# Softmax with the row maximum: scores on four banks, another bank order in the query bursts, the first 28 tiles normalized on GpSimd

## The chip, the cores and the metric

The kernel runs on one core of a Trainium2 chip. The time is the device time of one execution in microseconds (us), as the median of several runs. The engines are named as in the profile: PE (TensorE's matmuls; PEld are its weight loads), DVE (VectorE), ACT (ScalarE), POOL (GpSimd), and SP, which issues most of the DMAs.

## The reference

A layer norm of x (2048 rows of 448) feeds an attention over the last 512 positions of a cached K and V (16 query heads of 256, two to each of 8 K/V heads) and a gated feed-forward block (1792 wide). The output is x + attention * silu(feed-forward).

```python
W = min(4096, max(256, Sk // 4))                       # 512
q = (x @ wq).reshape(B, Sq, Hq, Dh).transpose(0, 2, 1, 3)
k = jnp.repeat(k_cache[:, :, Sk - W:, :], rep, axis=1)
v = jnp.repeat(v_cache[:, :, Sk - W:, :], rep, axis=1)
scores = jnp.einsum("bhqd,bhkd->bhqk", q, k) * (Dh ** -0.5)
p = softmax(scores, axis=-1)
o = jnp.einsum("bhqk,bhkd->bhqd", p, v)
s = o.transpose(0, 2, 1, 3).reshape(B, Sq, Hq * Dh) @ wo
g = silu((gelu(x @ w_gate) * (x @ w_up)) @ w_down)
out = x_in + s * g                                     # x above is layernorm(x_in)
```

## The kernel before

The author's recorder `Rec` takes the instructions in program order, finds the dependencies by key and puts semaphore waits in front of an instruction where it needs them. Each engine runs its own instructions strictly in the recorded order; there is no scheduler. A PSUM bank is a key `("ps", b)`: who writes a bank waits for all earlier readers of it.

The 2048 rows are four blocks of 512. First comes the feed-forward for all four (`gate_up`, `down`), with the layer norm of the next block between; the last block's `down` is kept back and its 56 matmuls are spread as pieces over the first score tiles (the table `fill`). Then comes the attention: a loop over `i` from 0 to 63, one head of one block each (head i % 16 of block i // 16), and within it over four tiles `t` of 128 rows. Tile number n is 4 i + t.

In one turn of the inner loop, `scores(i, t)` multiplies 128 query rows with the 512 keys: two matmuls (L552) into one bank, 4 or 5 in turn. ACT takes the exponential straight from the bank, with the scale folded in, and sums the row (L556); DVE forms the reciprocal of the sum (L558) and multiplies the row by it (L559). The normalized tile, in one of 11 buffers `pr`, is transposed by a DMA issued from SP (`dmaT`) into `pT`. No row maximum is subtracted.

At t = 0 and 2, from tile 12 on, `values` (L574) multiplies an earlier head's transposed probabilities with V, about three heads behind, into bank 0, 1 or 6; a DVE copy (L581) moves the result to `oT`. At t = 1 and 3, from head 7 on, half of an output projection (`outproj`, L604) runs into bank 7, and after the second half DVE adds the bank to `acc` (L627; L625 for the first group of a block). When a block's last group is added, POOL multiplies with the gate `gy` and adds x (L631, L633). Three heads are other than the rest: at i = 18, 34 and 50 the values give way to the projection of a second row tile (bank 6), and at i = 22, 38 and 54 there is no projection. The last head of each block is folded (its V and its part of wo were multiplied beforehand, `vw`) and needs no `values`. The gate's tanh runs on ACT (L645) with two POOL steps (L646, L648) after heads 7, 9, 11 and 13 of a block.

The queries come in bursts: `q_burst` runs at tile t = 0 of head 3 (four heads) and of heads 7, 15, 23, 31, 39, 47 and 55 (eight heads), after that turn's scores and values. A burst of eight heads has eight parts, each for two heads and one half of the 256 columns. A part uses a pair of banks, s and s + 1, and has two phases: eight matmuls of 64 rows that run in pairs, and six more. PE's order puts the first phase of part n ahead of the second phase of part n - 1:

```python
for n in range(heads + 1):
    if n < heads:
        part(n, 0)
    if n:
        part(n - 1, 1)
```

After a part's second phase ACT copies both banks to `qT` in one instruction of 1024 columns (L527). The pairs are taken as `2 * (n % 3)` in the bursts of eight: banks 0 and 1, 2 and 3, 4 and 5, 0 and 1, and so on. In the burst at head 3 the pairs are 0, 2, 1, 0.

Of the kernel before, what the change touches and what calls it, by code (L numbers as in the profile page):

```python
# [5 lines left out]
ACT = mybir.ActivationFunctionType  # L6
ALU = mybir.AluOpType
BF16 = mybir.dt.bfloat16
F32 = mybir.dt.float32

LN_EPS = 1e-5
P = 128
# [132 lines left out]
def bass_recurrent_scan__sliding_block_cached__geglu_ffn__prompt_kernel(nc, A_x, A_k, A_v, A_wq, A_wo, B_x, B_wg, B_wu, B_wd, out):  # L145
    _, S, D = A_x.shape
# [3 lines left out]
    W = min(4096, max(256, Sk // 4))  # L150
    F = B_wg.shape[1]
    QC, TPC, HP, KF = 512, 4, 64, 3
# [5 lines left out]
    scale = float(Dh) ** -0.5  # L158
# [3 lines left out]
    with es:  # L162
        off = [16512]

        def sb(name, shape, dt, at=None):
            n = 4 if dt == F32 else 2
            for x in shape[1:]:
                n *= x
            if at is None:
                at = off[0]  # L170
                off[0] += (n + 31) // 32 * 32
            return R.place(name, shape, dt, at), at + (n + 31) // 32 * 32

        ident, _ = sb("ident", [P, P], BF16)
        small, _ = sb("small", [P, 4], F32)
        stats, _ = sb("stats", [P, NT, 6], F32)
        mv, _ = sb("mv", [P, NT, 2], F32)
        std, _ = sb("std", [P, NT], F32)
        rstd, _ = sb("rstd", [P, NT], F32)
        den, _ = sb("den", [P, 16], F32)  # L180
        rden, _ = sb("rden", [P, 16], F32)

        xnT, _ = sb("xnT", [P, NQC, KF + 1, QC], BF16)
        gy, _ = sb("gy", [P, NT, D], BF16)
        kT, _ = sb("kT", [P, Hkv, NE, W], BF16)
        V, _ = sb("V", [P, NJ, Hkv, Dh], BF16)

        wq, _ = sb("wq", [P, KF, Hq, Dh], BF16)
        wq6, _ = sb("wq6", [P, Hq // 2, Dh], BF16)
        wo, _ = sb("wo", [P, Hq * NE, D], BF16)  # L190

        vw, _ = sb("vw", [P, NJ, D], BF16)
        gu_at = off[0]

        wg, _ = sb("wg", [P, KF, F], BF16)
        wu, _ = sb("wu", [P, KF, F], BF16)
        wgu6, x_at = sb("wgu6", [P, F], BF16)
        x4, _ = sb("x4", [P, NT, D], BF16)
        NX = 4
        xn2, d_at = sb("xn2", [P, NX, D + HP], BF16)  # L200
        wd, _ = sb("wd", [P, NF, D], BF16)
# [13 lines left out]
        pr = []  # L215
# [17 lines left out]
        NPR = len(pr)  # L233
        psum = es.enter_context(nc.psum_tensor("ps", [P, 8 * 512], F32))

        def bank(b, n=512):
            return psum[:, b * 512:b * 512 + n]
# [6 lines left out]
        act = lambda *a, **k: R.op("scalar", *a, **k)  # L244
        dve = lambda *a, **k: R.op("vector", *a, **k)
        pool = lambda *a, **k: R.op("gpsimd", *a, **k)
# [4 lines left out]
        def dmaT(dst, src, w=(), r=(), after=(), lane=None):  # L251
# [9 lines left out]
             r=[("ident",)], w=[("ident",)])  # L261
# [245 lines left out]
        NI = NQC * Hq  # L507
        NG = NI // 4

        def q_slot(i):  # L510

            p = i // 2
            p = p if p < 3 else (p - 3) % NQP
            return qT[p], "qT%d" % p, i % 2

        def q_burst(i0, heads):

            c, h0 = divmod(i0, Hq)

            def part(n, ph):  # L520
                hp, e_ = divmod(n, 2)
                s, h = 2 * (n % 3 if heads == 8 else (0, 2, 1, 0)[n] if i0 else (n + 2) % 4), h0 + 2 * hp
                buf, name, _ = q_slot(i0 + 2 * hp)
                two_blocks(ph, c, s, [wq[:, :, h + m, e_ * P:(e_ + 1) * P] for m in range(2)],
                           wq6[:, h // 2, e_ * P:(e_ + 1) * P], wq_keys)
                if ph:
                    act(lambda e: e.activation(  # L527
                        buf[:, :, e_, :], psum[:, s * 512:(s + 2) * 512].rearrange("p (a q) -> p a q", a=2), ACT.Copy),
                        r=[("ps", s), ("ps", s + 1)], w=[(name, e_)])

            for n in range(heads + 1):
# [5 lines that stand above are left out]
        def folded(i):  # L537
            return i % Hq == Hq - 1

        def p_slot(i):  # L540

            n = (i - i // Hq) % NPT
            return (pTf, ("pT", "f")) if folded(i) else (pT[:, n, :, :], ("pT", n))

        def scores(i, t):
            g, n = (i % Hq) // 2, i * TPC + t
            b, s = 4 + n % 2, n % NPR
            buf, name, a = q_slot(i)

            def run(e):  # L550
                for k in range(NE):
                    ins = e.matmul(bank(b), lhsT=buf[:, a, k, t * P:(t + 1) * P], rhs=kT[:, g, k, :],  # L552
                                   start=k == 0, stop=k == NE - 1)
                return ins
            pe(run, r=[("kT", g), (name, 0), (name, 1)], w=[("ps", b)])
            act(lambda e: e.activation(pr[s][:, :], bank(b), ACT.Exp, scale=scale, accum_out=den[:, s:s + 1]),  # L556
                r=[("ps", b)], w=[("pr%d" % s,), ("den", s)])
            dve(lambda e: e.reciprocal(rden[:, s:s + 1], den[:, s:s + 1]), r=[("den", s)], w=[("rden", s)])  # L558
            dve(lambda e: e.tensor_scalar(pr[s][:, :], pr[s][:, :], rden[:, s:s + 1], None, op0=ALU.mult),  # L559
                r=[("pr%d" % s,), ("rden", s)], w=[("pr%d" % s,)])  # L560
            dst, key = p_slot(i)
            dmaT(dst[:, :, t * P:(t + 1) * P], pr[s][:, :], r=[("pr%d" % s,)], w=[(*key, t)], lane="p%d" % s)

        def values(i, e_):
            g = (i % Hq) // 2
            idx = (i % 4) * NE + e_
            src, pkey = p_slot(i)
            at = 2 * i + e_ + 6

            b = (0, 6, 0, 6, 0, 1, 6, 6)[at % 8] if at < 2 * NI else (0, 6, 1, 0, 6, 1)[at - 2 * NI]  # L570

            def run(e):
                for j in range(NJ):
                    ins = e.matmul(bank(b), lhsT=V[:, j, g, e_ * P:(e_ + 1) * P], rhs=src[:, j, :],  # L574
                                   start=j == 0, stop=j == NJ - 1)
                return ins
            pe(run, r=[(*pkey, t) for t in range(TPC)] + ([("V", j) for j in range(NJ)] if g < Hkv - 1 else [("V", "f")]),
               w=[("ps", b)])
            dst, key = oT[(i // 4) % 2][:, idx, :], ("oT%d" % ((i // 4) % 2), idx)
            if i < NI - 2:  # L580
                dve(lambda e: e.tensor_copy(dst, bank(b)), r=[("ps", b)], w=[key])  # L581
            else:
                act(lambda e: e.activation(dst, bank(b), ACT.Copy), r=[("ps", b)], w=[key])

        def n_pieces(G):
            return 3 * NE + NJ if folded(4 * G + 3) else 4 * NE
# [55 lines left out]
        def silu(n):  # L642

            s = n % 2
            act(lambda e: e.activation(tmp[:, s, :], gy[:, n, :], ACT.Tanh, scale=0.5), r=[("gy", n)], w=[("tmp", s)])  # L645
            pool(lambda e: e.tensor_scalar(tmp[:, s, :], tmp[:, s, :], 1.0, 0.5, op0=ALU.add, op1=ALU.mult),  # L646
                 r=[("tmp", s)], w=[("tmp", s)])
            pool(lambda e: e.tensor_tensor(gy[:, n, :], tmp[:, s, :], gy[:, n, :], ALU.mult),  # L648
                 r=[("tmp", s), ("gy", n)], w=[("gy", n)])


        for c in range(NQC):
            lead = 6 if c == 0 else 2
            for f in range(NF + 1):
# [4 lines left out]
                t = (f - lead) // 2  # L659
# [17 lines left out]
        load_xr(0)  # L677

        fill = {}
        for d, slots in ((0, range(0, 4)), (1, range(4, 12)), (2, range(13, 17)), (3, range(17, 21))):  # L680
            for n, s in enumerate(slots):
                fill[s] = d, range(n * NF // len(slots), (n + 1) * NF // len(slots))
        pv = [(i, e_) for i in range(NI) if not folded(i) for e_ in range(NE)]
        outs = [(G, t) for G in range(NG) for t in range(TPC)]
        for i in range(NI):
            for t in range(TPC):
                scores(i, t)
                if 4 * i + t in fill:
                    down(NQC - 1, *fill[4 * i + t])

                early = i >= Hq and i % Hq == 2
                if t % 2 == 0 and early:
                    n = n_pieces(outs[1][0])
                    outproj(*outs[1], range(n * t // 4, n * (t + 2) // 4), b=6)
                elif t % 2 == 0 and 4 * i + t >= 12:
                    values(*pv.pop(0))
                if 7 <= i and t % 2 and not (i >= Hq and i % Hq == 6):
                    n = n_pieces(outs[0][0])
                    outproj(*outs[0], range(n * (t - 1) // 4, n * (t + 1) // 4))
                    if t == TPC - 1:  # L700
                        del outs[0:1 + early]
                if t == 0 and (i == 3 or i % 8 == 7) and i + 1 < NI:
                    q_burst(i + 1, 4 if i == 3 else 8)
            if i % Hq in (7, 9, 11, 13):
                silu(i // Hq * TPC + (i % Hq - 7) // 2)

        for what in "vvovovo":
            if what == "v":
# [38 lines left out]
```

## Time and profile before

| what | value |
|---|---|
| median of 3 runs | 558.33 us (558.14 to 558.38) |
| the profiled execution | 558.53 us, of it 556.7 us span |
| last block's feed-forward ends, attention begins | 133.5 us |
| first tile's exponential; tile 12's; tile 28's; tile 255's | 134.77; 144.60; 170.23; 537.47 us |
| a burst of eight heads, 170.9 to 183.1 us | PE 12.20, DVE 1.13, ACT 6.77 us busy of 12.20 |
| the run of 31 tiles after it, 183.1 to 222.9 us | PE 39.49, DVE 31.41, ACT 25.00, POOL 6.40 us busy of 39.80 |
| the granted TensorE clock | 1.00 throughout |
| exponential, L556, 128x512 | 598 ns, 256 of them |
| batch statistics, L335, 128x448 on DVE | 619 ns |
| POOL product of two tiles, L631, 128x448 | 1035 ns |

The page's times are those of one profiled execution. A duration is that of one instruction from start to end; on one engine the end of one overlaps with the start of the next, so that an engine's durations can add up to more than it needs. "Idle before" says how long an engine stood still before the instructions of a group, and which instruction ended it. The windows of the table are sums of busy time of the engine in that stretch.

### The profile page before, as it was taken

How to read it: one execution, taken by the hardware profiler on the slowest of the kernel's cores; microseconds unless marked ns; L12 is line 12 of the kernel's file. 1: busy time of each engine (PE TensorE's matmuls, PEld its weight loads, DVE VectorE, ACT ScalarE, POOL GpSimd, SP SyncE). 2: the span in 40 equal slices, each digit the busy share in tenths (PEclk: the TensorE clock that was granted, in tenths of full speed). 3: DMA queues.
4: the chain of work that ended last, by engine and by line, in shares of the span. 5: the costliest groups of instructions: out<-in, count | busy, mean ns of one | idle time of the engine just before them, and what ended most of it. 6: DMA issues, size and time to landing. Idle time of an engine off the chain costs nothing.

```text
span 556.7 us, 9892 instructions
## 1 busy us (share of the span) xinstructions
PE 550.0 (99%) x3517; PEld 261.4 (47%) x3550; DVE 313.7 (56%) x822; ACT 296.1 (53%) x689; POOL 88.6 (16%) x125
## 2 busy tenths in 40 slices
PE   9999999999999999999999999999999999999997
PEld 6444444444444444444444444444444444444445
DVE  5535436043463678077728744772688077628774
ACT  5333324237655666555575556556665655575640
POOL 0131213200000121002301110131121002311134
PEclk9999999999999999999999999999999999999999
DMA  8883555952444354245554552556355245635461
GB/s 237 287 141 70 134 86 96 265 114 54 97 86 76 58 100 96 53 85 96 128 76 93 104 92 42 96 99 139 66 96 102 41 87 103 138 64 105 95 96 52
DMA packets 165440, 57.65 MB, mean 104 GB/s; under 512 B 155648, under 2 KB 162304, under 8 KB 165392
## 3 DMA queue, kind: packets, MB, share of 16 engines
q1 hardware_dynamic: 162048, 44.64, 42.5%
q0 software_dynamic: 3040, 12.16, 8.1%
q8 instruction: 28, 0.46, 0.3%
q10 hardware_dynamic: 304, 0.22, 0.2%
q14 instruction: 20, 0.16, 0.1%
HBM read 17.92 MB, written 1.84 MB: 35 GB/s over the span
## 4 chain that ended last, share of the span: by engine, by line
PE 98%; DMA 1%; issue 1%; SPq 0%; DVE 0%
PE ps L472 33%; PE ps L552 20%; PE ps L574 19%; PE ps L604 19%; PE ps L496 8%; DMA V<-in_A_v_cache_dram 1%; PE ps L400 0%; PE ps L357 0%; PE ps L387 0%; PE ps L347 0%; SPq L249 0%; PE ps L359 0%; DVE tmp L615 0%; DVE xr L617 0%
## 5 line engine op out<-in xcount | busy, mean ns | idle before, releaser
L556 ACT ACTIVATE pr<-ps 128x512 bf16<-128x512 f32 x256 | 152.6, 598 | 120.1 <-PE ps L552 118.8
L552 PE MATMUL ps<-kT,qT 128*128 128x512 bf16 x487 | 145.2, 379 | 2.3 <-issue 1.4
L558 DVE RECIPROCAL rden<-den 128x1 f32<-128x1 f32 x256 | 41.4, 162 | 154.1 <-ACT pr L556 139.6
L574 PE MATMUL ps<-pT,V 128*128 128x512 bf16 x472 | 121.9, 379 | 0.4
L559 DVE TENSOR_SCALAR pr<-pr,rden 128x512 bf16<-128x512 bf16 x256 | 106.1, 414 | 9.0
L604 PE MATMUL ps<-wo,oT 128*128 128x448 bf16 (+1 forms) x498 | 110.9, 346 | 0.0
L472 PE MATMUL ps<-xnT,wq 64*128 64x512 bf16 x896 | 98.3, 376 | 0.0
L527 ACT ACTIVATE qT<-ps 128x1024 bf16<-128x1024 f32 x64 | 64.6, 1023 | 43.3 <-PE ps L472 43.0
L472 PE MATMUL ps<-xnT,wu 64*128 64x512 bf16 x336 | 82.3, 376 | 0.0
L472 PE MATMUL ps<-xnT,wg 64*128 64x512 bf16 x336 | 82.0, 376 | 0.0
L581 DVE CAST oT<-ps 128x512 bf16<-128x512 f32 x118 | 80.5, 683 | 0.7 <-PE ps L574 0.6
L490 DVE TENSOR_TENSOR actT<-ps,hb 128x512 bf16<-128x512 f32 x56 | 38.5, 692 | 65.9 <-ACT hb L489 61.7
L552 PEld LDWEIGHTS ps<-kT,qT 128*128 128x128 bf16 x512 | 49.2, 98 | 55.4 <-issue 4.0
L574 PEld LDWEIGHTS ps<-pT,V 128*128 128x128 bf16 x480 | 47.0, 98 | 56.3
L604 PEld LDWEIGHTS ps<-wo,oT 128*128 128x128 bf16 x498 | 48.4, 98 | 48.6 <-DVE acc L627 1.0
L472 PEld LDWEIGHTS ps<-xnT,wq 64*128 64x128 bf16 x896 | 43.0, 94 | 54.5 <-DVE rden L558 1.7
L489 ACT ACTIVATE hb<-ps 128x512 bf16<-128x512 f32 x56 | 33.1, 594 | 38.6 <-PE ps L472 38.5
L556 ACT ACTIVATION_READ_ACCUMULATOR pr<-ps 128x1 f32 x256 | 50.3, 196 | 0.0
L496 PE MATMUL ps<-wd,actT 128*128 128x448 bf16 x224 | 46.2, 353 | 0.0
L472 PEld LDWEIGHTS ps<-xnT,wg 64*128 64x128 bf16 x336 | 31.3, 94 | 20.5 <-issue 1.1
L472 PEld LDWEIGHTS ps<-xnT,wu 64*128 64x128 bf16 x336 | 31.3, 94 | 19.9
L646 POOL TENSOR_SCALAR tmp<-tmp 128x448 f32<-128x448 f32 x16 | 9.0, 565 | 198.1 <-ACT tmp L645 198.1
(60 smaller groups left out, 264.7 us busy)
## 6 DMA issues: line engine op xcount, KB each, us to landing
pT<-pr SPq DMA_TRANSPOSE x240, 2.5
wq<-in_A_wq_dram POOLq DMA_DIRECT2D x14, 256.0 KB, 3.7
wo<-in_A_wo_dram POOLq DMA_DIRECT2D x3, 896.0 KB, 8.3
V<-in_A_v_cache_dram POOLq DMA_DIRECT2D x4, 448.0 KB, 7.0
xr<-in_A_x_dram POOLq DMA_DIRECT2D x4, 448.0 KB, 4.1
wd<-in_B_w_down_dram SPq DMA_DIRECT2D x1, 1568.0 KB, 14.3
x<-in_A_x_dram SPq DMA_DIRECT2D x3, 448.0 KB, 7.5
out_dram<-xr POOLq DMA_DIRECT2D x3, 448.0 KB, 3.7
```

What stands on the lines that cost most here:

```text
L472: ins = e.matmul(bank(s + m)[:, q0:q1], lhsT=lhsT, rhs=xnT[lo:lo + HP, c, k, q0:q1], start=ph == 0 and k == 0, stop=ph == 1 and k == KF - 1)
L489: act(lambda e: e.activation(hb[:, h, :], bank(s), ACT.Gelu_apprx_tanh), r=[("ps", s)], w=[("hb", h)])
L490: dve(lambda e: e.tensor_tensor(actT[:, f, :], bank(s + 1), hb[:, h, :], ALU.mult), r=[("ps", s + 1), ("hb", h)], w=[("actT", f)])
L496: pe(lambda e, f=f: e.matmul(bank(b, D), lhsT=actT[:, f, t * P:(t + 1) * P], rhs=wd[:, f, :], start=f == 0, stop=f == NF - 1), r=[("actT", ...
L527: act(lambda e: e.activation(buf[:, :, e_, :], psum[:, s * 512:(s + 2) * 512].rearrange("p (a q) -> p a q", a=2), ACT.Copy), r=[("ps", s), ...
L552: ins = e.matmul(bank(b), lhsT=buf[:, a, k, t * P:(t + 1) * P], rhs=kT[:, g, k, :], start=k == 0, stop=k == NE - 1)
L556: act(lambda e: e.activation(pr[s][:, :], bank(b), ACT.Exp, scale=scale, accum_out=den[:, s:s + 1]), r=[("ps", b)], w=[("pr%d" % s,), ("de ...
L558: dve(lambda e: e.reciprocal(rden[:, s:s + 1], den[:, s:s + 1]), r=[("den", s)], w=[("rden", s)])
L559: dve(lambda e: e.tensor_scalar(pr[s][:, :], pr[s][:, :], rden[:, s:s + 1], None, op0=ALU.mult), r=[("pr%d" % s,), ("rden", s)], w=[("pr%d ...
L574: ins = e.matmul(bank(b), lhsT=V[:, j, g, e_ * P:(e_ + 1) * P], rhs=src[:, j, :], start=j == 0, stop=j == NJ - 1)
L581: dve(lambda e: e.tensor_copy(dst, bank(b)), r=[("ps", b)], w=[key])
L604: ins = e.matmul(bank(b, D)[:, lo:hi], lhsT=lhsT, rhs=rhs, start=idx == 0, stop=idx == n8 - 1)
```

## The change

Each score tile now has its row maximum taken by DVE from the bank, negated (`nmax`), and ACT's exponential gets it as its bias; the scale moves into the copy of the queries. The reciprocal and the multiplication of a tile are taken out of `scores` into `normalize`, which is called one tile later (LAG = 1). For the first 28 tiles POOL does the multiplication. The scores use three banks (4, 5, 2) up to tile 12 and then four (2 to 5) in turn. The copies of the attention values go to ACT, except the odd half of heads 0 to 6. The pairs of banks in the bursts and the slots of the kept-back `down` pieces have another order.

```diff
+        nmax, _ = sb("nmax", [P, 16], F32)
...
-                s, h = 2 * (n % 3 if heads == 8 else (0, 2, 1, 0)[n] if i0 else (n + 2) % 4), h0 + 2 * hp
+                s, h = 2 * ((2, 0, 1, 2, 0, 2, 1, 0)[n] if heads == 8 else (0, 1, 2, 0)[n] if i0 else (n + 2) % 4), h0 + 2 * hp
...
-                        buf[:, :, e_, :], psum[:, s * 512:(s + 2) * 512].rearrange("p (a q) -> p a q", a=2), ACT.Copy),
+                        buf[:, :, e_, :], psum[:, s * 512:(s + 2) * 512].rearrange("p (a q) -> p a q", a=2), ACT.Copy, scale=scale),
...
+        LAG, FIRST = 1, 7 * TPC
+
+        def s_bank(n):
+            return (4, 5, 2)[n % 3] if n <= 3 * TPC else 2 + (n + 1) % 4
+
         def scores(i, t):
             g, n = (i % Hq) // 2, i * TPC + t
-            b, s = 4 + n % 2, n % NPR
+            b, s = s_bank(n), n % NPR
...
-            act(lambda e: e.activation(pr[s][:, :], bank(b), ACT.Exp, scale=scale, accum_out=den[:, s:s + 1]),
-                r=[("ps", b)], w=[("pr%d" % s,), ("den", s)])
+            dve(lambda e: e.tensor_reduce(nmax[:, s:s + 1], bank(b), mybir.AxisListType.X, ALU.max, negate=True),
+                r=[("ps", b)], w=[("nmax", s)])
+            act(lambda e: e.activation(pr[s][:, :], bank(b), ACT.Exp, bias=nmax[:, s:s + 1], accum_out=den[:, s:s + 1]),
+                r=[("ps", b), ("nmax", s)], w=[("pr%d" % s,), ("den", s)])
+
+        def normalize(i, t):
+            s = (i * TPC + t) % NPR
             dve(lambda e: e.reciprocal(rden[:, s:s + 1], den[:, s:s + 1]), r=[("den", s)], w=[("rden", s)])
-            dve(lambda e: e.tensor_scalar(pr[s][:, :], pr[s][:, :], rden[:, s:s + 1], None, op0=ALU.mult),
-                r=[("pr%d" % s,), ("rden", s)], w=[("pr%d" % s,)])
+            if i * TPC + t < FIRST:
+                pool(lambda e: e.tensor_tensor(pr[s][:, :], pr[s][:, :], rden[:, s:s + 1].to_broadcast([P, W]), ALU.mult),
+                     r=[("pr%d" % s,), ("rden", s)], w=[("pr%d" % s,)])
+            else:
+                dve(lambda e: e.tensor_scalar(pr[s][:, :], pr[s][:, :], rden[:, s:s + 1], None, op0=ALU.mult),
+                    r=[("pr%d" % s,), ("rden", s)], w=[("pr%d" % s,)])
             dst, key = p_slot(i)
             dmaT(dst[:, :, t * P:(t + 1) * P], pr[s][:, :], r=[("pr%d" % s,)], w=[(*key, t)], lane="p%d" % s)
...
-            if i < NI - 2:
+            if i * TPC < FIRST and e_:
                 dve(lambda e: e.tensor_copy(dst, bank(b)), r=[("ps", b)], w=[key])
             else:
                 act(lambda e: e.activation(dst, bank(b), ACT.Copy), r=[("ps", b)], w=[key])
...
-        for d, slots in ((0, range(0, 4)), (1, range(4, 12)), (2, range(13, 17)), (3, range(17, 21))):
+        for d, slots in ((0, range(0, 4)), (1, range(4, 8)), (2, range(8, 12)), (3, range(13, 23))):
...
             for t in range(TPC):
+                n = i * TPC + t
                 scores(i, t)
+                if n >= LAG:
+                    normalize(*divmod(n - LAG, TPC))
...
+        for n in range(NI * TPC - LAG, NI * TPC):
+            normalize(*divmod(n, TPC))
```

## The prediction

> **What bounds the kernel now.** I read the page's busy times first, then its chain of waits, then the groups by line, then the timelines of one burst of query projections (L472, L527) and of one stretch of score tiles.
>
> ```profile
> span 556.7 us, 9892 instructions
> ...
> PE 550.0 (99%) x3517; PEld 261.4 (47%) x3550; DVE 313.7 (56%) x822; ACT 296.1 (53%) x689; POOL 88.6 (16%) x125
> ...
> PE 98%; DMA 1%; issue 1%; SPq 0%; DVE 0%
> ...
> L558 DVE RECIPROCAL rden<-den 128x1 f32<-128x1 f32 x256 | 41.4, 162 | 154.1 <-ACT pr L556 139.6
> L559 DVE TENSOR_SCALAR pr<-pr,rden 128x512 bf16<-128x512 bf16 x256 | 106.1, 414 | 9.0
> L527 ACT ACTIVATE qT<-ps 128x1024 bf16<-128x1024 f32 x64 | 64.6, 1023 | 43.3 <-PE ps L472 43.0
> L581 DVE CAST oT<-ps 128x512 bf16<-128x512 f32 x118 | 80.5, 683 | 0.7 <-PE ps L574 0.6
> ```
>
> PE is the chain: 98% of it, with every other engine near half busy. A busy share alone does not prove a dense PE, so I checked the distance from one matmul's start to the next: 216 ns for 512 columns and 189 ns for 448, in the run of score tiles without exception other than a few missing records. So the change can hardly win time; it can lose it wherever PE, which works strictly in order, meets a bank that is not free. Three places matter.
>
> First, the bursts. Eight parts of queries are projected in a row; each is a first half (8 matmuls in 4 pairs, 0.863 us) and, after the next part's first half, a second half (3 pairs, 0.648 us), then one copy of 1024 columns on ACT empties its two banks.
>
> ```profile
> 381.14 1.02 ACT L527 ACTIVATE qT<-ps 128x1024 bf16<-128x1024 f32 x1 [2.51 <-PE ps L472]
> 382.65 1.02 ACT L527 ACTIVATE qT<-ps 128x1024 bf16<-128x1024 f32 x1 [0.49 <-PE ps L472]
> 384.16 1.02 ACT L527 ACTIVATE qT<-ps 128x1024 bf16<-128x1024 f32 x1 [0.49 <-PE ps L472]
> ```
>
> The copies come every 1.51 us = 0.863 + 0.648 and ACT idles 0.49 us before each. The trace has the second half's last pair starting at 380.72 us and the next pair at 380.94, so the copy (381.14) begins 0.205 us after PE could take up the next thing, and ends 1.229 us after it.
>
> Second, what PE does when it must wait for such a copy; there is one such place already, after the small burst of the fourth head:
>
> ```profile
> 150.97 1.94 ACT L527 ACTIVATE qT<-ps 128x1024 bf16<-128x1024 f32 x2 [0.49 <-PE ps L472]
> ...
> 152.04 0.30 PEld L496 LDWEIGHTS ps<-wd,actT 128*128 128x128 bf16 x3 [0.43 <-ACT qT L527]
> 152.05 0.74 PE L496 MATMUL ps<-wd,actT 128*128 128x448 bf16 x3
> ```
>
> The first of the two merged copies ends at 151.99 (150.97 + 1.02) and the matmul that writes its bank starts at 152.05: release to matmul takes about 0.05 us.
>
> Third, VectorE in a run of score tiles, where it has room today:
>
> ```profile
> 341.70 0.35 DVE L559 TENSOR_SCALAR pr<-pr,rden 128x512 bf16<-128x512 bf16 x1
> 341.97 0.68 DVE L581 CAST oT<-ps 128x512 bf16<-128x512 f32 x1
> ...
> 343.23 0.62 DVE L627 TENSOR_TENSOR acc<-ps,acc 128x448 f32<-128x448 f32 x1
> ```
> ```profile
> 364.57 0.77 DVE L559 TENSOR_SCALAR pr<-pr,rden 128x512 bf16<-128x512 bf16 x1
> 365.26 0.68 DVE L581 CAST oT<-ps 128x512 bf16<-128x512 f32 x1
> 365.86 0.15 DVE L558 RECIPROCAL rden<-den 128x1 f32<-128x1 f32 x1
> ```
>
> Durations overlap, so I count slots, start to start with nothing waited for: 0.27 us for the multiply (341.70 to 341.97), 0.60 for a 512-column read from PSUM (365.26 to 365.86), 0.20 for a reciprocal and the wait of the multiply behind it, 0.53 for the 448-column accumulation (L627).
>
> **The change part by part.** The sum is against the profiled execution: 558.53 us, 1.83 above its span. The median of the runs shown, 558.33, is 0.2 lower; I carry that as nothing.
>
> *The maximum.* 256 reductions of 128x512 from PSUM on DVE, none in the trace. Nearest row: the CAST, same shape and source. Lower bound of its slot 0.52 (512 elements at the slope between the 448- and 512-column CASTs, 618 and 683 ns: 65 ns for 64), upper 0.68 (the CAST's duration without overlap). I take 0.60, the CAST's slot, since the batch statistics (L335), also a reduction, take 619 ns for 448, what the 448-column CAST takes.
>
> *What DVE loses in exchange.* 111 of the 118 output CASTs of L581 move to ACT; DVE keeps seven, the odd halves of heads 0 to 6. A head of four tiles then costs DVE 4 x (0.60 + 0.20 + 0.27) + 0.53 = 4.81 us. PE takes 4.97 for a head in a run (two tiles 2.485, the starts of L552 at 341.41 and 343.89). So it fits with 0.16 to spare. I also walked the order of the queue, for a lateness hidden in the mean. The accumulation that frees bank 7 stands behind the reduction and the multiply of the tile before; by the slots it starts 0.51 us after PE ends the projection, ends at 1.13, and PE wants the bank at about 1.5 (today it starts at 0.63 and PE does not wait). At 0.60 it costs nothing; cover left 0.3 us. Should the reduction take 0.68, a head is 5.13, 0.16 over PE, and the runs (seven of about eight heads, each restarting with an empty queue after a burst) lose 7 x (8 x 0.16 - 0.3) = 6.9 us. At 0.52 nothing changes.
>
> In the head with two accumulations (18, 34, 50) and the head before a burst without any projection (22, 38, 54) DVE is over PE by 0.2 and 0.8 us; four score banks take that up, but the burst behind the second starts on banks 4 and 5, whose last exponential by my walk ends within 0.2 us of its turn. I put 0.2 each, 3 x 0.2 = 0.5 with the smaller ones, bounds 0 and 3.
>
> [...]
>
> *ACT.* Today exponential to exponential takes 0.48 + 0.09 us. A bias read from a tile adds 93 ns (L373, one column with such a bias, 296 ns; the one without, L675, 203). So two tiles cost ACT 2 x 0.66 + one output copy 0.48 (the slot of L489) = 1.80 of 2.485 us. Hidden; the exponential now waits for the reduction, some 0.7 us, but the bank is wanted four tiles later instead of two. The scale moved into the copy of L527 is the same instruction.
>
> *The multiply one tile later; the first 28 on POOL.* 28 products of 512 columns at 1035 x 512/448 = 1.18 us (L631); bounds 0.65 (L646, one input, 565 ns scaled alike) and 1.6 (with the 0.42 by which a product of POOL and a multiply of DVE hold each other up in the line above). With the gap of 0.08 it is 35 us beside 37 us of PE (133.5 to 170.9). The first values, at tile 12, have their last product done some 1.6 us before at the middle price, hidden; at 1.6 the cover is 0.3. Its transposes wait on SP behind it in order: SP issues one in 1.21 us and a tile takes 1.24, as today. Tile 28 of each burst is normalized only behind the burst; its head is wanted nine tiles later.
>
> POOL's products hold up the multiply today (0.77 instead of 0.35 in the line above, L631 running). [...]
>
> *The banks of the bursts: here it costs.* The pairs of banks were taken in the order 0 1 2 0 1 2 0 1: a part reuses the pair of the part three before, whose copy has 1.51 us, and needs 1.229 + 0.05 = 1.28. Now the order is 2 0 1 2 0 2 1 0. Sixth part on pair 2, as the fourth: only two apart. In PE's order the sixth part's first half stands directly behind the fourth part's second half, so that the whole copy lies bare: PE waits 1.28 us. PE has nothing else in its queue to put there. Seven bursts of eight parts (heads 7, 15, ..., 55): 7 x 1.28 = 8.9 us. Bounds: 7 x 1.229 = 8.6 with no release time, 7 x 1.43 = 10.0 with 0.2, the longest that a load of L552 waited for an exponential. The other parts stay three or more apart.
>
> In the burst of four at head 3 the order becomes 0 1 2 0, and the next score tile takes bank 4, of the third part. Its first matmul moves from 151.52 (by its weight load; the record of the matmul is missing) to about 152.05, and the 0.09 us of today's wait, shown above, falls away: 0.45 us.
>
> *Down pieces* (L496) are spread otherwise over the first 23 tiles, the same 56 matmuls: nothing.
>
> Sum: 8.9 + 0.45 + 0.5 = 9.9; 558.5 + 9.9 = 568.4 us.
>
> **Rivals.** (a) DVE becomes the bound of the runs as well, if reduction or reciprocal take longer slots than I took: for it, only 0.16 us of 4.97 are spare and POOL's holds come on top; against, the CAST's row. At 0.68: 568.4 + 6.9 = 575.3. (b) The burst's wait is smaller than worked out, because something I did not see frees the pair earlier: 560 to 566. Nothing in the profile speaks for it. (c) Not slower: four score banks and the freed DVE take away the waits that PE has today. Its weight loads waited 1.7 us for L558, 2.3 for L627 and 0.7 for L556, and PE idles 2.3 us before L552 and 0.4 before L574; taking those 2.7 away gives 555.8. It decides only if the sixth part waits under 0.3 us a burst, that is if the copy of 1.02 us did not stand between; against it, PE's order. (d) The reuse does not bite at all and the rest is as summed: 558.5 + 0.45 + 0.5 = 559.5; that the copy of 1.02 us lies bare speaks against it as against (c).
>
> **How the numbers follow.** Forecast, 567 to 570.5: 0.62. (a), 570.5 to 578: 0.24. (b): 0.08. (d): 0.04. (c): 0.02. Predicted 568.4. The range leaves out (c), (d), most of (b) and the upper end of (a): 565.8 to 577. A difference under 0.2% (1.1 us) cannot be told from none: faster 0.02, same 0.03, slower 0.95.
>
> **What will show it.** Right: in each burst one copy of queries comes 2.8 us after the one before instead of 1.51, PE's loads wait for L528's copies seven times for 9 us in all, PE's busy time stays at 550 and its share falls to 97%; reductions at about 683 ns, exponentials at 690, DVE about 70% busy (313.7 - 76 for the CASTs - 12 for POOL's share + 175). Wrong: bursts still 12.2 us long; or gaps of PE inside the runs with the accumulation (L643) or the exponential as their releaser, which is rival (a).

## The result, and the profile after

The changed kernel takes 572.54 us (572.1 to 572.91, five runs) against 558.22 of the kernel before measured beside it: a ratio of 1.0256, 95% interval 1.0241 to 1.0271. The profiled execution's span grew by 14.1 us, from 556.7 to 570.8.

The page of the changed kernel, busy times, chain and the groups that answer to those of before (in a group: times it ran, busy us in all, mean ns, idle time ahead and who ended it):

```profile
span 570.8 us, 10398 instructions
...
PE 556.0 (97%) x3550; PEld 261.9 (46%) x3550; DVE 369.5 (65%) x939; ACT 369.6 (65%) x800; POOL 117.1 (21%) x153
...
PE 82%; DVE 13%; ACT 2%; issue 1%; DMA 1%; POOL 0%; ACTq 0%
...
L563 DVE TENSOR_REDUCE nmax<-ps 128x1 f32<-128x512 f32 x256 | 175.0, 684 | 111.1 <-PE ps L559 107.7
L565 ACT ACTIVATE pr<-ps,nmax 128x512 bf16<-128x512 f32 x256 | 175.9, 687 | 69.7 <-PE ps L590 35.4
...
L575 DVE TENSOR_SCALAR pr<-pr,rden 128x512 bf16<-128x512 bf16 x228 | 86.7, 380 | 8.1
L528 ACT ACTIVATE qT<-ps 128x1024 bf16<-128x1024 f32 x64 | 64.5, 1023 | 36.0 <-PE ps L473 35.3
...
L599 ACT ACTIVATE oT<-ps 128x512 bf16<-128x512 f32 x113 | 66.4, 588 | 4.6 <-PE ps L590 4.5
```

PE does the same matmuls in a longer span, so its share falls to 97%, and the chain, which was 98% PE, now runs through DVE for 13%. That share is no price: 13% of the span is 74 us, and the span grew by 14. Which waits are PE's own is told by the waits of its weight loads (us in all, times, longest):

```profile
PEld ps L473 <- ACT qT L528: 11.3, 7, 1.6
PEld ps L590 <- ACT oT L599: 5.6, 8, 1.1
...
PEld ps L620 <- DVE acc L641: 1.9, 3, 0.7
...
PEld ps L559 <- ACT qT L528: 1.0, 1, 1.0
PEld ps L590 <- issue: 0.9, 1, 0.9
```

None of these five rows was there before. Where nothing holds it, a load starts about 0.2 us ahead of its matmul in this trace (0.214 us in the median of L473, L559 and L590, 0.188 of L620), so these rows overstate what the matmuls lose, by some 0.33 us a wait; I therefore also took the distance from one matmul's start to the next in the trace, less the 216 or 189 ns that is the most frequent distance for 512 or 448 columns. What is lost that way, and was not lost before, adds up to 14.1 us, the difference of the two spans to within some tenths (the attention of this execution also starts 0.25 us earlier than before):

| where PE waits | places | us |
|---|---|---|
| sixth part of a burst of eight, for the copy of the fourth (L528) | 7 | 8.95 |
| attention values (L590) for the copy out of bank 6 (L599) | 8 | 2.93 |
| projections of heads 8 to 10 for the accumulation out of bank 7 (L641) | 3 | 0.91 |
| attention values of head 62, for a transposed tile | 1 | 0.66 |
| first score tile behind the burst of head 3 (0.54, less 0.10 that were waited before) | 1 | 0.44 |
| entry into the bursts of heads 23, 39 and 55 | 3 | 0.22 |
| sum | | 14.11 |

The first burst of eight, in the timeline of the changed kernel (start, duration, engine, line, operation, idle before and who ended it):

```profile
176.63 1.02 ACT L528 ACTIVATE qT<-ps 128x1024 bf16<-128x1024 f32 x1 [0.49 <-PE ps L473]
178.14 1.02 ACT L528 ACTIVATE qT<-ps 128x1024 bf16<-128x1024 f32 x1 [0.49 <-PE ps L473]
179.22 2.70 PEld L473 LDWEIGHTS ps<-xnT,wq 64*128 64x128 bf16 x28 [1.61 <-ACT qT L528]
179.22 2.98 PE L473 MATMUL ps<-xnT,wq 64*128 64x512 bf16 x26 [1.12 <-ACT qT L528]
180.95 1.02 ACT L528 ACTIVATE qT<-ps 128x1024 bf16<-128x1024 f32 x1 [1.78 <-PE ps L473]
```

The fourth part's copy runs from 178.14 to 179.16; PE stands still through it and starts the sixth part at 179.22. The next copy comes 2.81 us later instead of 1.51.

### The profile page after: what moved, and what is told of

It reads as the page before. It is cut to its first block, busy times and chain, and to the rows that moved or that the text cites. A ratio compares the mean times of both kernels' runs of the same rounds, so it can differ in the third digit from the quotient of the medians.

```text
span 570.8 us, 10398 instructions
## 1 busy us (share of the span) xinstructions
PE 556.0 (97%) x3550; PEld 261.9 (46%) x3550; DVE 369.5 (65%) x939; ACT 369.6 (65%) x800; POOL 117.1 (21%) x153
## 4 chain that ended last, share of the span: by engine, by line
PE 82%; DVE 13%; ACT 2%; issue 1%; DMA 1%; POOL 0%; ACTq 0%
PE ps L473 32%; PE ps L559 15%; PE ps L590 15%; PE ps L620 12%; PE ps L497 7%; DVE nmax L563 7%; DVE pr L575 3%; ACT qT L528 1%; DVE acc L641 1%; DVE acc L643 1%; DVE rden L570 1%; PE ps L348 1%; ACT oT L599 1%; DMA pT<-pr 1%; DVE oT L597 0%
## 5 line engine op out<-in xcount | busy, mean ns | idle before, releaser
L563 DVE TENSOR_REDUCE nmax<-ps 128x1 f32<-128x512 f32 x256 | 175.0, 684 | 111.1 <-PE ps L559 107.7
L565 ACT ACTIVATE pr<-ps,nmax 128x512 bf16<-128x512 f32 x256 | 175.9, 687 | 69.7 <-PE ps L590 35.4
L559 PE MATMUL ps<-kT,qT 128*128 128x512 bf16 x512 | 150.9, 379 | 0.5 <-ACT qT L528 0.5
L590 PE MATMUL ps<-pT,V 128*128 128x512 bf16 x480 | 123.1, 379 | 2.1 <-ACT oT L599 1.4
L620 PE MATMUL ps<-wo,oT 128*128 128x448 bf16 (+1 forms) x498 | 111.0, 346 | 0.4 <-DVE acc L641 0.4
L473 PE MATMUL ps<-xnT,wq 64*128 64x512 bf16 x896 | 99.5, 376 | 7.9 <-ACT qT L528 7.8
L575 DVE TENSOR_SCALAR pr<-pr,rden 128x512 bf16<-128x512 bf16 x228 | 86.7, 380 | 8.1
L528 ACT ACTIVATE qT<-ps 128x1024 bf16<-128x1024 f32 x64 | 64.5, 1023 | 36.0 <-PE ps L473 35.3
L473 PE MATMUL ps<-xnT,wu 64*128 64x512 bf16 x336 | 82.3, 376 | 0.0
L473 PE MATMUL ps<-xnT,wg 64*128 64x512 bf16 x336 | 82.0, 376 | 0.0
L559 PEld LDWEIGHTS ps<-kT,qT 128*128 128x128 bf16 x512 | 49.4, 98 | 55.8 <-issue 3.4
L590 PEld LDWEIGHTS ps<-pT,V 128*128 128x128 bf16 x480 | 46.3, 98 | 60.7 <-ACT oT L599 5.6
L473 PEld LDWEIGHTS ps<-xnT,wq 64*128 64x128 bf16 x896 | 44.0, 94 | 62.8 <-ACT qT L528 11.3
L620 PEld LDWEIGHTS ps<-wo,oT 128*128 128x128 bf16 x498 | 48.4, 98 | 49.5 <-DVE acc L641 1.9
L599 ACT ACTIVATE oT<-ps 128x512 bf16<-128x512 f32 x113 | 66.4, 588 | 4.6 <-PE ps L590 4.5
L565 ACT ACTIVATION_READ_ACCUMULATOR pr<-ps,nmax 128x1 f32 x256 | 50.4, 197 | 0.0
L647 POOL TENSOR_TENSOR tmp<-acc,gy 128x448 f32<-128x448 f32 x16 | 16.6, 1035 | 149.3 <-DVE acc L643 141.2
L473 PEld LDWEIGHTS ps<-xnT,wg 64*128 64x128 bf16 x336 | 31.3, 94 | 20.5 <-issue 1.1
```

The costliest lines, as they stand in the source:

```text
L473: ins = e.matmul(bank(s + m)[:, q0:q1], lhsT=lhsT, rhs=xnT[lo:lo + HP, c, k, q0:q1], start=ph == 0 and k == 0, stop=ph == 1 and k == KF - 1)
L528: act(lambda e: e.activation(buf[:, :, e_, :], psum[:, s * 512:(s + 2) * 512].rearrange("p (a q) -> p a q", a=2), ACT.Copy, scale=scale), ...
L563: dve(lambda e: e.tensor_reduce(nmax[:, s:s + 1], bank(b), mybir.AxisListType.X, ALU.max, negate=True), r=[("ps", b)], w=[("nmax", s)])
L565: act(lambda e: e.activation(pr[s][:, :], bank(b), ACT.Exp, bias=nmax[:, s:s + 1], accum_out=den[:, s:s + 1]), r=[("ps", b), ("nmax", s)], ...
L620: ins = e.matmul(bank(b, D)[:, lo:hi], lhsT=lhsT, rhs=rhs, start=idx == 0, stop=idx == n8 - 1)
```

## The experiments

Each version was timed beside runs of the kernel before. "Pair 3" is banks 6 and 7.

**The bank order alone, on the kernel before.** This tells whether the wait needs the maximum at all.

```diff
-                s, h = 2 * (n % 3 if heads == 8 else (0, 2, 1, 0)[n] if i0 else (n + 2) % 4), h0 + 2 * hp
+                s, h = 2 * ((2, 0, 1, 2, 0, 2, 1, 0)[n] if heads == 8 else (0, 2, 1, 0)[n] if i0 else (n + 2) % 4), h0 + 2 * hp
```

> The kernel before with nothing but the changed order of bank pairs in the bursts of eight (2 0 1 2 0 2 1 0). Theory (bank reuse two parts apart lays one copy of queries bare in each of seven bursts): 558.2 + 7 x 1.28 = 567.2 us, and PE's distance of 1.50 us from one projection matmul to the next seven times. Rival (the wait is only there because VectorE, loaded with the maximum, has to catch up in the burst): no maximum here, so 558 to 559 us.

Measured: 568.22 us beside 558.45, ratio 1.0176 (1.0161 to 1.0191). In its waits of PE's loads the row of the changed kernel stands again, to the digit:

```profile
PEld ps L472 <- ACT qT L527: 11.3, 7, 1.6
...
PEld ps L472 <- ACT pr L556: 3.5, 7, 0.6
```

By matmul starts the seven waits are 8.97 us. The second row is a small wait of the first part, which in this kernel begins on the bank of an exponential just started (0.13 us of a matmul at four of the seven). Another 1.1 us of the profiled execution lies ahead of the feed-forward, whose first matmul starts at 11.46 us instead of 10.31; this start lies between 9.7 and 11.5 us in the profiles of this case, and so spans of two profiled executions can differ by 1 us through it alone. The waits of the two rows add up to 9.5 us; the medians differ by 9.8. The rival falls.

**The sixth part on a fourth pair of banks, on the changed kernel.** The values' bank 6 and the projections' bank 7 are not in use in the middle of a burst.

```diff
-                s, h = 2 * ((2, 0, 1, 2, 0, 2, 1, 0)[n] if heads == 8 else ...
+                s, h = 2 * ((2, 0, 1, 2, 0, 3, 1, 0)[n] if heads == 8 else ...
```

> The changed kernel with the sixth part of each burst of eight on banks 6 and 7, a fourth pair. Theory: the seven waits of 1.28 us go, 572.5 - 9.0 = 563.6 us, and all other gaps of PE stay. Rival (VectorE sets the pace of the runs and the burst only gives it time to catch up): the wait reappears in the runs, 570 us or more.

Measured: 563.72 us, ratio 1.0092 (1.0075 to 1.0108). The row of L473 waiting for L528 is gone from the waits. The others are what they were, but for the wait at the end, which grows from 0.66 to 0.92 us by matmul starts:

```profile
PEld ps L590 <- ACT oT L599: 5.6, 8, 1.1
...
PEld ps L620 <- DVE acc L641: 1.9, 3, 0.7
```

So the bursts' 8.8 us come off as a block, and the remaining 5 us belong to something else.

**No maximum.** The reduction is left out and `nmax` is set to zero once for each buffer, so this version does not subtract the maximum.

```diff
-            dve(lambda e: e.tensor_reduce(nmax[:, s:s + 1], bank(b), mybir.AxisListType.X, ALU.max, negate=True),
-                r=[("ps", b)], w=[("nmax", s)])
+            if n < NPR:
+                dve(lambda e: e.memset(nmax[:, s:s + 1], 0.0), w=[("nmax", s)])
```

> The changed kernel without the reduction: the bias is read from a tile set to zero once, so exponential, bias, banks, copies and the later multiplication stay. Theory: the bursts' 9.0 us and the 0.45 us behind the burst of head 3 stay, the 2.9 us of attention values that wait for bank 6 and the 0.9 us in heads 8 to 10 go, the 0.7 us at the end may stay: 567.7 to 568.5 us. Rival (the maximum itself is what costs): 558 to 561 us.

Measured: 567.67 us, ratio 1.0165 (1.015 to 1.0181). The bursts' row stays at 11.3 us and 7 times, the rows of L590 and L620 are gone, the wait at the end too (the forecast had left that open). The maximum and everything that depends on its time thus cost 572.5 - 567.7 = 4.9 us, the two places with burst banks the other 9.4.

**All copies of attention values back on VectorE**, in the version with the fourth pair, to test the count of DVE's slots.

```diff
-            if i * TPC < FIRST and e_:
+            if i < NI - 2:
```

> The version with the fourth pair, but all copies of the attention values back on VectorE as before the change (except those of the last two heads). A head of a run then costs VectorE 4.81 + 2 x 0.60 = 6.0 us of slots against 4.97 of PE: about 1.0 x 8 - 0.5 us a run, seven runs, some 50 us: 605 to 622 us. Rival (VectorE's slots overlap more than I count, the move of the copies was not needed): under 575 us.

Measured: 605.55 us, ratio 1.0843 (1.0821 to 1.0865), at the lower end of the forecast. PE's loads wait for DVE's accumulation, as a late DVE would have it:

```profile
PEld ps L620 <- DVE acc L643: 29.1, 29, 1.4
PEld ps L620 <- DVE acc L641: 15.6, 12, 1.4
PEld ps L473 <- DVE pr L575: 10.4, 9, 2.0
```

On the page DVE is busy for only 71% of this version's span (428.6 of 603.9 us), though it sets the pace of every run of score tiles; a share over the whole span does not tell that. A share within a run tells little more: from 308 to 345 us DVE is busy for 36.11 of 37.00 us here, and for 36.50 of 38.00 us in the run from 184 to 222 us of the version with all repairs (below), where PE loses nothing in the run. The sum of the slots does tell it, 6.0 us a head against PE's 4.97 here and 4.81 there: in the trace of this version the waiting projections follow each other every 5.99 us (five heads from 312.07 to 342.00 us).

**Four repairs, one added to the other**, each aimed at one row of the table. First the second of two values that follow each other on bank 6 goes to bank 1:

```diff
-            b = (0, 6, 0, 6, 0, 1, 6, 6)[at % 8] if at < 2 * NI else (0, 6, 1, 0, 6, 1)[at - 2 * NI]
+            b = (0, 6, 0, 6, 0, 1, 6, 1)[at % 8] if at < 2 * NI else (0, 6, 1, 0, 6, 1)[at - 2 * NI]
```

> As the version with the fourth pair, and the second of two attention-value results that follow each other on bank 6 goes to bank 1. Theory (the copy now stands on ScalarE behind an exponential that waits for the maximum, 2.9 us over eight places): 563.7 - 2.9 = 560.8 us, up to 561.3 if a part of the 0.75 us at head 11 turns into a wait for the accumulation. Rival (VectorE is late anyway, the bank is only where it shows): 563 us or more.

Measured: 560.85 us, ratio 1.0053 (1.0037 to 1.0069). What it removes is seen in the changed kernel's timeline, here at head 11:

```profile
206.37 0.69 ACT L565 ACTIVATE pr<-ps,nmax 128x512 bf16<-128x512 f32 x1 [0.64 <-PE ps L559]
206.96 0.19 ACT L565 ACTIVATION_READ_ACCUMULATOR pr<-ps,nmax 128x1 f32 x1
207.05 0.59 ACT L599 ACTIVATE oT<-ps 128x512 bf16<-128x512 f32 x1
```
```profile
207.69 0.55 PEld L590 LDWEIGHTS ps<-pT,V 128*128 128x128 bf16 x4 [1.08 <-ACT oT L599]
```

The copy of the last values stands on ACT behind an exponential, which cannot start before DVE has reduced its tile (205.61 to 206.29 here; the row names PE, but the last matmul of this tile started at 205.39). The copy ends at 207.64 and the next values, on the same bank, begin at 207.69.

Then DVE keeps only the copies of heads 0 to 3:

```diff
-            if i * TPC < FIRST and e_:
+            if i < 4 and e_:
```

> In addition only the odd halves of heads 0 to 3 are copied by VectorE instead of heads 0 to 6: those of heads 4 to 6 run three heads later, inside the first run. Theory (three copies of 0.60 us put VectorE over PE there and the projection waits for its accumulation): the 0.9 us before heads 8 to 10's projections goes, 559.9 us (559.6 to 560.3). Rival (those waits come from the gate's work on GpSimd): no change, 560.8.

Measured: 560.29 us, ratio 1.0035 (1.0021 to 1.0049). The median fell by 0.56 rather than 0.9, but the two intervals overlap, so the times alone do not show it. The matmul distances do: the gaps before the projections in the first run are gone, while the one at the end, 1.20 us in the version before this, has grown to 1.42 in this profiled execution. Each repair so far brought PE to the last values sooner, and part of what it won was waited there. What filled DVE in the first run, in the timeline of the changed kernel:

```profile
198.30 0.69 DVE L597 CAST oT<-ps 128x512 bf16<-128x512 f32 x1
198.90 0.68 DVE L563 TENSOR_REDUCE nmax<-ps 128x1 f32<-128x512 f32 x1
199.50 0.15 DVE L570 RECIPROCAL rden<-den 128x1 f32<-128x1 f32 x1
199.69 0.35 DVE L575 TENSOR_SCALAR pr<-pr,rden 128x512 bf16<-128x512 bf16 x1
199.96 0.62 DVE L641 COPY acc<-ps 128x448 f32<-128x448 f32 x1
```
```profile
200.63 0.49 PEld L620 LDWEIGHTS ps<-wo,oT 128*128 128x128 bf16 x4 [0.74 <-DVE acc L641]
```

No gap between DVE's instructions, a copy of head 6 among them, and the projection waits for the accumulation at the end of that queue.

Then the values of head 62, the last, come behind two projections; so far the first half of them came behind one:

```diff
-        for what in "vvovovo":
+        for what in "vvoovvo":
```

> In addition the last attention values stand one projection later (two projections before them instead of one). Theory (they wait for the transposed probabilities of head 62, which are later by the maximum and the later multiplication): the 0.7 to 0.9 us at the end goes, 559.1 us (558.8 to 559.4). Rival: the wait moves to the last projections, 559.9.

Measured: 558.91 us, ratio 1.0013 (1.0004 to 1.0021). What waited there before, in the changed kernel's timeline:

```profile
553.15 1.68 PE L620 MATMUL ps<-wo,oT 128*128 128x448 bf16 x8
555.33 1.02 PE L590 MATMUL ps<-pT,V 128*128 128x512 bf16 x4 [0.50 <-DMA pT<-pr]
```

In this version's trace the wait is gone, 1.42 us by matmul starts; the median fell by 1.38.

And last the burst of head 3:

```diff
-... (0, 1, 2, 0)[n] if i0 ...
+... (0, 1, 3, 0)[n] if i0 ...
```

> In addition the third part of the burst at head 3 goes to banks 6 and 7, so that the next score tile doesn't wait for its copy. Theory: 0.45 us less a new wait of 0.1 for bank 7: 558.7 us, the time of the kernel before (558.4) within 0.1%. Rival (something of the maximum stays in the runs): 559.1 or more.

Measured: 558.77 us, ratio 1.0011 (1.0002 to 1.002). The last step's 0.14 is inside the scatter of the two medians; in the trace the wait of the score tile (0.54) is gone. The page of this version:

```profile
span 556.7 us, 10372 instructions
...
PE 549.8 (99%) x3517; PEld 263.9 (47%) x3550; DVE 367.5 (66%) x936; ACT 370.8 (67%) x803; POOL 117.1 (21%) x153
```

The span is that of the kernel before, 556.7 us, with all 256 reductions still in it. The start of the feed-forward varies, so a closer measure is the time from the last matmul ahead of the attention to the last matmul of all: 425.87 us with the fourth pair, then 423.13, 422.43, 421.01 and 420.69 with one repair after the other, beside 420.39 in the kernel before. What is left, 0.3 us in the traces and 0.6 in the medians, is in part the entry into three bursts, which no repair touched. No version measured here is faster than the kernel before.

**GpSimd's 28 products**, taken back to VectorE in the version with all four repairs:

```diff
-            if i * TPC + t < FIRST:
+            if i * TPC + t < 0:
```

> As the version with all four repairs (558.8), but VectorE normalizes the first 28 tiles too. By slots VectorE then takes 1.07 us a tile there, beside PE's 1.09 up to tile 12, 1.13 to tile 22 and 0.86 to tile 28. Theory (the four banks and the burst behind take up the lateness): 558.8 to 560 us, so GpSimd's part is worth 1.2 us at most. Rival (GpSimd's part is what keeps the first stage whole): 562 us or more.

Measured: 561.01 us, ratio 1.0052 (1.0035 to 1.0068): 2.2 us, more than the theory's 1.2 and less than the rival's 3.2. The place is the forecast's, the size is not. Score tiles wait for banks just before the first burst of eight:

```profile
168.96 0.11 PEld L559 LDWEIGHTS ps<-kT,qT 128*128 128x128 bf16 x2 [0.58 <-ACT pr L565]
170.01 0.11 PEld L559 LDWEIGHTS ps<-kT,qT 128*128 128x128 bf16 x2 [0.94 <-ACT pr L565]
```

By matmul starts these two cost 0.25 and 0.61 us. PE then waits 0.71 us more at the entry into the burst, 0.36 inside it, and 0.18 in the burst of head 3: 2.1 us in all. The forecast had the four banks and the burst take up the whole lateness.

**The scores on two banks**, as before the change, in the version with all four repairs:

```diff
-            return (4, 5, 2)[n % 3] if n <= 3 * TPC else 2 + (n + 1) % 4
+            return 4 + n % 2
```

> As the version with all four repairs, but the scores on banks 4 and 5 in turn as before the change. A bank is then wanted after two tiles (2.49 us), and reduction, exponential and their releases take some 2.0 us from the end of the score, 2.5 us where the accumulation stands before the reduction; and each burst begins on a bank whose exponential has just begun (1.2 us). Theory (the four banks are needed): 572 to 581 us. Rival (the wait for the maximum stays hidden with two banks too): under 561 us.

Measured: 580.32 us, ratio 1.0398 (1.0382 to 1.0413). The waits of its loads:

```profile
PEld ps L559 <- ACT pr L565: 41.4, 112, 1.1
PEld ps L473 <- DVE pr L575: 9.2, 6, 1.7
```

Four banks are what lets the exponential wait for the maximum: without them 112 score tiles wait. The second row is the entry into the bursts, which begin on these same two banks. It names the multiply, but at the second burst, whose first matmul starts at 229.00 us, the multiply ended at 228.46 and the last exponential at 228.77; the bank waits for the exponential.

## Why the prediction was right, and where it was not, point by point

It forecast 568.4 us, with a chance of 0.62 for 567 to 570.5; measured were 572.5, above that and in the stretch of rival (a), to which it gave 0.24. The sign, the leading cause and its size were right. The sum came out 4 us short, because three waits that it had put at nothing cost 4.5 us; that the range as a whole, up to 577, still held the time is owed to the room left for rival (a), another mechanism, and is luck.

- *The bursts, 8.9 us:* measured 8.95 in the changed kernel, 8.97 alone on the kernel before, and 8.8 come off with a fourth pair. Copy, release and distance were all in the rows of before.
- *Behind the burst of head 3, 0.45 us:* 0.44.
- *The maximum on DVE:* the reduction takes 684 ns and 0.60 us of slot, as taken from the CAST; a head fits in 4.81 of 4.97 us, and with the repairs the whole change costs 0.6 us (558.77 beside 558.19).
- *The rest, "0.2 each, 3 x 0.2 = 0.5":* this step failed. The three bursts it named cost 0.22, but there were three more places, which cost 4.5 us; the 4.7 together lie above the upper bound of 3 that it gave. Under *ACT* I wrote "Hidden" and thought of the score banks alone; the copies of the attention values, which I had just moved to ACT, stand there behind an exponential that waits for the maximum, and the values use bank 6 twice running in heads 11, 19, 27, 35, 43, 51, 59 and 63 (2.93 us). Under *What DVE loses in exchange* I left the seven copies that DVE keeps out of the head's 4.81 us; those of heads 4 to 6 run three heads later, inside the first run, where 0.16 us a head is all the room there is (0.91). And under *The multiply one tile later* I followed the tiles to a head nine tiles on, but not at the end, where head 62 is wanted sooner (0.66).
- *The 28 products on POOL:* 1.18 us forecast from a product of 448 columns, 1041 ns measured for 512; hidden, as said. 26 of the reductions ran beside these products and took 671 to 692 ns, the others 671 to 693. That a product and a multiply hold each other up, as the upper bound of 1.6 had it, was not shown: in the trace of before the 40 multiplies beside a product of two tiles are longer (406 to 969 ns, 352 to 355 with GpSimd idle), but all 48 of these products take 1029 to 1037 ns.
- *Rival (a)* named the range in which the time fell, but not its cause: reduction and reciprocal had the slots of the forecast (0.60 and 0.19 us measured, 0.60 and 0.20 forecast), and VectorE set the pace only in heads 8 to 10 and, at the entry, in three bursts, 1.1 us together. The sign given for it, gaps inside the runs with the accumulation as releaser, did appear, at three places (L641). Rivals (b), (c) and (d) were wrong: nothing freed the pair earlier, and no waits of before were won back.
- *The signs:* one copy 2.81 us after the one before (2.8 said), seven waits, PE's share 97%, exponentials at 687 ns. PE's busy time is 556.0 and not 550: the page of before lacks 33 of the 3550 matmul records, and ahead of a wait a matmul counts with its whole 379 ns instead of the 216 ns to the next. DVE's share is 65%, not 70: I added durations (their sum rose from 335 to 413 us), but the page counts overlapping instructions once, and closer together they overlap more (busy 314 to 369 us).

## What to carry to other kernels

Where an engine works in order and is full, write down for each bank who empties it, how long that takes from the last write, and how much of that engine's own work lies between one use of the bank and the next; an order of buffers that looks balanced can have one reuse a step too close (here 1.28 us in each of seven bursts). An instruction moved to another queue inherits the waits of what stands in front of it there (here 2.93 us over eight copies of attention values on ACT): price it by its neighbours, not by the free time of its engine. And follow a shifted stage (values three heads behind the scores) to the time at which it really runs.

## What the runs showed of the hardware that was not expected

GpSimd's product of a bf16 tile with a broadcast column takes 1041 ns for 512 columns, while its products of two tiles of 448 columns, one of them fp32, take 1035 ns in the same profile: it does not go by the number of columns alone. The prediction had scaled by columns, to 1.18 us.
